# The low halves of the second product's input lie at other distances from their high halves

## Chip, core and metric

The kernel runs on one core of a Trainium2 chip. The metric is the device time of one execution in microseconds. Of the kernel before there are two timed executions, 2079.07 and 2080.16 us, median 2079.61.

## What is computed

Attention with four sink positions and a window of 128 (batch 4, 8 heads, 768 positions, 64 wide) gives a matrix `x` of 3072 tokens by 512. It goes through a soft mixture of 8 experts, whose weights per token come from eight rounds of normalizing rows and columns:

```python
def _moe_ref(x, w_gate, w1, w2):          # x: 3072 x 512, w1: 8 x 512 x 1024, w2: 8 x 1024 x 512
    ...                                    # P: 3072 x 8, weights of the experts
    for e in range(E):
        h = np.maximum(x @ w1[e], 0.0)     # first product
        ye = h @ w2[e]                     # second product
        out += P[:, e:e + 1] * ye
```

Nearly all of the time goes into the two products of the mixture.

## The kernel before

**Tiling.** After the attention the 3072 tokens are taken in three parts of 1024. The code counts them 0, 1 and 2; here they are parts 1, 2 and 3. An expert's 1024 inner columns are taken in four units of 256, so a part has 8 x 4 = 32 units. Both products go by Strassen's scheme on blocks of 2 by 2: seven products `M1` to `M7` in place of eight, with sums of blocks before and after.

**Halves.** A value in float32 is kept as two numbers of the type that TensorE multiplies at full rate: a high half, which is the value cast, and a low half, which is the value less its high half. A product then takes three matmuls: high by high, high by low, low by high. A tile that holds both is `[128, 2, n]`: along each partition first the n high numbers and then the n low ones. With n = 512 in float32 the low half starts 2048 bytes after the high one.

**Parts 2 and 3.** `first2` (from L1392) makes the first product of a unit. Each of the seven `M` is six matmuls of 512 columns (line L902, in `product`), whose weights come from the queue `W1q` and whose streaming operand is one of the token forms `B11`, `B21`, `B22`, `T1` to `T4`. ScalarE copies a result out of its bank (L1411), VectorE adds another to it (L1415) and takes the positive part times the expert's weight (L1416, L1445), GpSimd makes three sums and differences (L1434, L1438, L1439, L1449). That gives the seven forms of the second product's input: `A11`, `A12`, `A22`, `S1` to `S4`, each 128 partitions by 512 tokens.

`form` (L1418) gives each form a tile `hf` of the pool `hq`, which has 16 buffers and is the last pool opened on its side of the on-chip memory. `piece` (L926) writes it: ScalarE casts the source into the high half (L928), and one step later VectorE subtracts this high half from the source into the low half (L931). A part makes 32 x 7 forms, both parts 448.

`second2` (from L1456) makes the second product. For each group of two units, each `M` and each of its two halves of output columns `k`, it has three matmuls a unit (L1467); the streaming operand is a half of `hf`, the weights come from `W2q`:

```python
for j, (a, w, n) in enumerate((a, w, n) for n in group for a, w in ((0, 0), (0, 1), (1, 0))):
    nc.tensor.matmul(o, lhsT=W2Q[part, n, m][:, a, k * P:(k + 1) * P], rhs=F[part, n, H_OF[m]][:, w, :],
```

`w` = 0 is the high half and `w` = 1 the low one, so of three matmuls the second streams a low half. A result goes to VectorE (L1481), which adds it to a sum in on-chip memory, or stays in a bank of its own (`held`) over several groups.

**Order.** The order is written out by hand: a unit's steps are listed in `STEPS2`, and `at(n, f)` puts an operation n steps later. A form is written in one unit and read in later ones.

**Part 1** has the same two products with other tiles: L902 with weights `W1f`, and L1152, whose streaming operand is a half of the weights `W2f`. Before all of it stands the attention, beside which the first expert's plain products run (L638, L652).

One place of the attention is used below. The scores' keys lie in `KQ`, a tile `[P, 2, NP, CW + 2 * P]` with NP = 2 and rows of 260 + 256 = 516 floats; L498 streams the first 260 (or 132) floats of such a row:

```python
KQ = [att1.tile([P, 2, NP, CW + 2 * P], F32R, name=f"KQ{hh}") for hh in range(2)]
    for j, (a, c) in enumerate(terms):         # ((0, 0), (0, 1), (1, 0))
        for r in range(2):
            rows = slice(r * D, (r + 1) * D)
            nc.tensor.matmul(..., lhsT=Q[rows, a, pr, :], rhs=K[rows, c, pr, 0:w], ...)
```

So L498 goes in pairs (`r`), one matmul for each half of the partitions. L473 and L474 write the high and low halves of `KQ` from the transposed keys and queries, 512 elements a partition in four blocks of 128.

Of the kernel before, what the change touches and what calls it, by code (L numbers as in the profile page):

```python
# [2 lines left out]

# [7 lines left out]
F32R = mybir.dt.float32r  # L11
# [5 lines left out]
P = 128  # L17
# [221 lines left out]
def tile_sink_attention_moe(ctx: ExitStack, tc: tile.TileContext, q, k, v, wg, w1, w2, out):  # L239
# [14 lines left out]
    HT = NPART // 2  # L254
# [128 lines left out]
    for hh in range(2):  # L383
        t = att2.tile([P, NP, CW + 2 * P], F32, name=f"KQF{hh}")
# [514 lines left out]
    def product(ps, w1, x, start, stop):  # L899

        for j, (a, k, b) in enumerate(TERMS):
            nc.tensor.matmul(ps, lhsT=w1(a, k), rhs=x[:, b, k, :], start=(start and j == 0),  # L902
                             stop=(stop and j == len(TERMS) - 1), skip_group_check=not start)
# [9 lines left out]
    def at(steps, f):  # L913
        assert steps > 0
        due.setdefault(clock[0] + steps, []).append(f)
# [10 lines left out]
    def piece(dst, src, then=None):  # L926

        nc.scalar.copy(dst[:, 0], src)  # L928

        def low():  # L930
            low_ = nc.vector.tensor_sub(dst[:, 1], src, f32(dst[:, 0])).ins  # L931
            if clock[0] < 120:
                LATE[:] = [tc, low_]

        at(1, low)
        if then:
            at(3, then)
# [398 lines left out]
    with ExitStack() as p1:  # L1336
        pool_ = lambda name, bufs, **kw: p1.enter_context(tc.tile_pool(name=name, bufs=bufs, reuse_waits="tile", **kw))
        W1N, W2N = 8, 16
        w1p, pb, cp, wp, hp = pool_("w1q", W1N), pool_("pb", 2), pool_("cq", 1), pool_("wq", 6), pool_("hq", 16)
        ORDER = ["M2", "M1", "M5", "M3", "M6", "M7", "M4"]  # L1340
        units1 = [(e, u) for e in range(E) for u in range(NU)]
        NJ = len(units1)
# [3 lines left out]
        W2Q = {}  # L1346
        coming1 = iter([(part, n, m) for part, n in jobs1 for m in ORDER if (part, n, m) not in W1Q])
        first_ones = set(W1Q)

        def load_w1(k):  # L1350
            for _ in range(k):
                key = next(coming1, None)
                if key:
                    part, n, m = key
                    t = W1Q[key] = w1p.tile([P, 2, KH, P], F32R, name="W1q")
                    nc.sync.dma_start(f32(t).rearrange("p w k f -> p w (k f)"), w1s[units1[n]][:, FA[W1_OF[m]]])
# [28 lines left out]
        def load_form(m):  # L1385
            fm = READS[m]
            XF[fm] = (xpool if fm[0] == "B" else xtp).tile([P, 2, KH, HT], F32R, name=fm)
            nc.sync.dma_start(f32(XF[fm]), xfs[FORMS.index(fm)])

        F = {}  # L1390

        def first2(part, n):  # L1392

            PB = PBS[part, units1[n][0]]
            T = {}

            def run(m):
                c = "c2" if m in ("M2", "M5", "M3") else "c1"
                start = m in ("M2", "M1", "M5")
                if start:  # L1400
                    T[c] = ps0.tile([P, HT], F32, name=c)
                W = W1Q.pop((part, n, m))
                product(T[c], lambda a, k: W[:, a, k, :], XF[READS[m]], start, True)
                if (part, n, m) not in first_ones:
                    at(1, lambda: load_w1(1))
                if (part, n) == (1, NJ - 1):
                    at(1, lambda: load_form(m))

            def copied(m):
                t = T[m] = cp.tile([P, HT], F32, name=m)  # L1410
                nc.scalar.copy(t, T["c2"])  # L1411

            def summed(key, m, th):
                w = T[key] = wp.tile([P, HT], F32, name="w")
                nc.vector.tensor_add(w, T["c1"], T[m])  # L1415
                nc.vector.scalar_tensor_tensor(w, w, 0.0, PB[:, th], op0=ALU.max, op1=ALU.mult)  # L1416

            def form(steps, fm, src):  # L1418
                def f():
                    t = F[part, n, fm] = hp.tile([P, 2, HT], F32R, name="hf")  # L1420
                    piece(t, src)

                at(steps, f)

            def after(m):
                if m in ("M2", "M5", "M3"):
                    copied(m)
                elif m == "M1":
                    summed("A11", "M2", 0)
                    form(2, "A11", T["A11"])  # L1430
                elif m == "M6":
                    summed("A21", "M3", 1)
                    S3 = wp.tile([P, HT], F32, name="w")
                    nc.gpsimd.tensor_sub(S3, T["A11"], T["A21"])  # L1434
                    form(2, "S3", S3)
                elif m == "M7":
                    summed("A22", "M5", 1)
                    nc.gpsimd.tensor_add(T["A21"], T["A21"], T["A22"])  # L1438
                    nc.gpsimd.tensor_sub(T["A11"], T["A21"], T["A11"])  # L1439
                    form(2, "S1", T["A21"])  # L1440
                    form(3, "A22", T["A22"])
                    form(4, "S2", T["A11"])
                else:
                    w = wp.tile([P, HT], F32, name="w")
                    nc.vector.scalar_tensor_tensor(w, T["c1"], 0.0, PB[:, 0], op0=ALU.max, op1=ALU.mult)  # L1445
                    form(1, "A12", w)

                    k = 4 if n < 2 else 3
                    at(k, lambda: nc.gpsimd.tensor_sub(T["A11"], w, T["A11"]))  # L1449
                    form(k + 2, "S4", T["A11"])  # L1450

            return run, after
# [190 lines left out]
```

## Time and profile before

| | |
|---|---|
| timed executions | 2079.07 and 2080.16 us, median 2079.61 |
| profiled execution, span from first to last instruction | 2077.3 us |
| its own time outside the span | not given; the median of the timed ones is 2.3 us above the span |
| TensorE busy | 2060.9 us, 99% of the span |
| VectorE busy | 1462.4 us, 70% |
| ScalarE busy | 840.2 us, 40% |
| GpSimd busy | 713.7 us, 34% |
| L1467, matmuls of the second product in parts 2 and 3 | 1920 + 768 |
| L931 into `hf`, low halves | 448, 329.1 us |
| L928 into `hf`, high halves | 448, 265.3 us |

PE is TensorE's matmul, PEld its weight load, DVE VectorE, ACT ScalarE, POOL GpSimd. A matmul's duration in the trace overlaps with that of the next one, so its pace is read from starts: from the start of a group in the timeline to the start of the group after it, divided by the number in the group.

### The profile page before, as it was taken

The numbers are of one execution on the slowest core, as the hardware profiler recorded it, in microseconds if no ns is written. First come the engines' busy times: TensorE is split into PE (matmuls) and PEld (weight loads), VectorE is DVE, ScalarE is ACT, GpSimd is POOL, SyncE is SP. The second block draws the span as 40 slices with busy tenths as digits, with TensorE's granted clock in tenths as the row PEclk, the third lists the DMA queues.
The fourth block names the chain that finished last, engine by engine and source line by source line (L and its number), as shares of the span: only waits on it lengthen the run. The fifth ranks groups of instructions, "written<-read, shape, count | busy, mean of one in ns | idle before, by whom it ended". The sixth has DMA issues, their size and how long they took to land.

```text
span 2077.3 us, 31257 instructions
## 1 busy us (share of the span) xinstructions
PE 2060.9 (99%) x10407; PEld 1706.0 (82%) x10407; DVE 1462.4 (70%) x2732; ACT 840.2 (40%) x1787; POOL 713.7 (34%) x833
## 2 busy tenths in 40 slices
PE   8999999999999999999999999999999999999998
PEld 7888778888888888888888888888888888888887
DVE  6777688787877767756666666666666667666666
ACT  7877445444444444333323322332432232333222
POOL 7766523333333321322322232233332223222323
PEclk9999999999999999999999999999999999999999
DMA  7655269898989886766666666668766666666662
GB/s 178 161 118 120 85 211 323 288 319 291 315 282 323 289 274 223 280 211 197 199 203 198 204 205 191 202 207 334 224 208 194 200 205 191 207 203 202 197 193 83
DMA packets 397622, 453.78 MB, mean 218 GB/s; under 512 B 99664, under 2 KB 265744, under 8 KB 396560
## 3 DMA queue, kind: packets, MB, share of 16 engines
q1 hardware_dynamic: 397064, 451.57, 69.6%
q8 instruction: 85, 1.39, 0.3%
q14 instruction: 81, 0.66, 0.1%
q10 hardware_dynamic: 392, 0.16, 0.0%
HBM read 314.17 MB, written 137.46 MB: 217 GB/s over the span
## 4 chain that ended last, share of the span: by engine, by line
PE 96%; DVE 2%; ACT 1%; POOL 0%; issue 0%; DMA 0%; SPq 0%; DVEq 0%; ACTq 0%; POOLq 0%
PE c L902 42%; PE o L1467 21%; PE held L1467 8%; PE held L1152 7%; PE o L1152 7%; PE st L638 2%; PE st L652 2%; PE st L572 2%; PE st L498 2%; PE st L457 1%; PE st L530 1%; PE st L580 0%; DVE sc L508 0%; DVE st L507 0%; PE st L603 0%
## 5 line engine op out<-in xcount | busy, mean ns | idle before, releaser
L928 ACT CAST hf<-w 128x512 fp32r<-128x512 f32 x448 | 265.3, 621 | 562.2 <-POOL w L1434 299.7
L1467 PE MATMUL o<-hf,W2q 128*128 128x512 f32 x1920 | 472.0, 389 | 0.0
L1467 PEld LDWEIGHTS o<-hf,W2q 128*128 128x128 f32 x1920 | 360.0, 188 | 75.5 <-DVE acc L1481 0.9
L902 PE MATMUL c<-T,W1q 128*128 128x512 f32 x1530 | 388.8, 389 | 0.2 <-DVE w L1415 0.2
L931 DVE TENSOR_TENSOR hf<-w,hf 128x512 fp32r<-128x512 f32 x448 | 329.1, 763 | 75.6 <-ACT hf L928 68.0
L902 PEld LDWEIGHTS c<-T,W1q 128*128 128x128 f32 x1530 | 286.8, 188 | 60.7 <-DVE w L1415 0.9
L1481 DVE TENSOR_TENSOR acc<-o,acc 128x512 f32<-128x512 f32 x298 | 204.6, 687 | 169.9 <-PE o L1467 169.9
L902 PE MATMUL c<-B,W1q 128*128 128x512 f32 x1134 | 278.3, 389 | 0.0
L1434 POOL TENSOR_TENSOR w<-w 128x512 f32<-128x512 f32 x64 | 82.7, 1293 | 492.0 <-DVE w L1416 492.0
L902 PEld LDWEIGHTS c<-B,W1q 128*128 128x128 f32 x1134 | 212.5, 188 | 44.0
L1415 DVE TENSOR_TENSOR w<-c,M 128x512 f32<-128x512 f32 x192 | 132.2, 689 | 139.9 <-PE c L902 135.6
L1411 ACT COPY M<-c 128x512 f32<-128x512 f32 x192 | 112.8, 587 | 249.1 <-PE c L902 249.0
L1467 PE MATMUL held<-hf,W2q 128*128 128x512 f32 x768 | 194.8, 389 | 0.0
L1152 PE MATMUL held<-W2f,h 128*128 128x512 f32 x672 | 171.1, 390 | 0.0
L902 PE MATMUL c<-T,W1f 128*128 128x512 f32 x672 | 171.0, 390 | 0.1
L1152 PE MATMUL o<-W2f,h 128*128 128x512 f32 x672 | 170.5, 389 | 0.1
L1467 PEld LDWEIGHTS held<-hf,W2q 128*128 128x128 f32 x768 | 144.0, 188 | 29.8
L1449 POOL TENSOR_TENSOR w<-w 128x512 f32<-128x512 f32 x64 | 106.3, 1661 | 176.0 <-DVE hf L931 176.0
L1152 PEld LDWEIGHTS o<-W2f,h 128*128 128x128 f32 x672 | 126.0, 188 | 27.0 <-DVE acc L1159 0.9
L902 PEld LDWEIGHTS c<-T,W1f 128*128 128x128 f32 x672 | 125.8, 188 | 26.9 <-issue 0.5
L1152 PEld LDWEIGHTS held<-W2f,h 128*128 128x128 f32 x672 | 125.8, 188 | 26.4 <-DVE W2f L931 0.5
L961 POOL TENSOR_TENSOR r<-r 128x256 f32<-128x256 f32 x27 | 20.1, 745 | 367.8 <-ACT M L1115 231.4
(216 smaller groups left out, 2740.3 us busy)
## 6 DMA issues: line engine op xcount, KB each, us to landing
W2q<-w2s SPq DMA_DIRECT2D x448, 256.0 KB, 3.1
W1q<-w1s SPq DMA_DIRECT2D x444, 256.0 KB, 2.8
w1s<-W1f SPq DMA_DIRECT2D x56, 896.0 KB, 7.7
w2s<-WT SPq DMA_DIRECT2D x136, 256.0 KB, 3.2
r<-in_moe_w_dram SPq DMA_DIRECT2D x64, 512.0 KB, 5.5
w2s<-W2f SPq DMA_DIRECT2D x56, 256.0 KB, 5.7
PB<-psd SPq DMA_DIRECT2D x16, 512.0 KB, 4.0
w2s<-W2f SPq DMA_DIRECT2D x56, 128.0 KB, 7.8
```

What stands on the lines that cost most here:

```text
L498: nc.tensor.matmul(ps[hh * HH + 2 * pr + r][:, 0:w], lhsT=Q[rows, a, pr, :], rhs=K[rows, c, pr, 0:w], start=(j == 0), stop=(j == len(terms ...
L572: nc.tensor.matmul(O[r * D:(r + 1) * D, c], lhsT=x_[:, 2 * c + r], rhs=y_[:, 2 * c + r], start=(j == 0 and c == 0), stop=(j == len(ops) - ...
L902: nc.tensor.matmul(ps, lhsT=w1(a, k), rhs=x[:, b, k, :], start=(start and j == 0), stop=(stop and j == len(TERMS) - 1), skip_group_check=n ...
L928: nc.scalar.copy(dst[:, 0], src)
L931: low_ = nc.vector.tensor_sub(dst[:, 1], src, f32(dst[:, 0])).ins
L1152: nc.tensor.matmul(o, lhsT=h[c, th][:, a, off:off + P], rhs=W2F[n][:, w, c, :], start=(begin and c == 0 and j == 0), stop=(end and c == 1 ...
L1411: nc.scalar.copy(t, T["c2"])
L1415: nc.vector.tensor_add(w, T["c1"], T[m])
L1434: nc.gpsimd.tensor_sub(S3, T["A11"], T["A21"])
L1449: at(k, lambda: nc.gpsimd.tensor_sub(T["A11"], w, T["A11"]))
L1467: nc.tensor.matmul(o, lhsT=W2Q[part, n, m][:, a, k * P:(k + 1) * P], rhs=F[part, n, H_OF[m]][:, w, :], start=(j == 0 and (begin or not hol ...
L1481: nc.vector.tensor_add(sums[m, k], o, sums[m, k])
```

## The change

The tile of a form grows from 1024 to 1040 floats a partition, 4160 bytes in place of 4096, so that the 16 buffers of `hq` lie 4160 bytes apart. The low half begins 512, 516 or 520 floats after the high half, by turns from form to form in the order in which the forms are made. The high half still begins at the start of its buffer. The shapes of all operations on the halves remain 128 by 512, each of contiguous floats. No instruction is added, removed or moved on any engine, and the waits are the same. Tiles of other pools keep their places.

```diff
+        gaps = itertools.cycle((0, 4, 8))
+
+        def new_h():
+
+            gap = next(gaps)
+            t = hp.tile([P, 2 * HT + 16], F32R, name="hf")
+            return t[:, 0:2 * (HT + gap)].rearrange("p (w c) -> p w c", w=2)[:, :, 0:HT]
+
...
             def form(steps, fm, src):
                 def f():
-                    t = F[part, n, fm] = hp.tile([P, 2, HT], F32R, name="hf")
+                    t = F[part, n, fm] = new_h()
                     piece(t, src)
```

HT is 512.

## Rows read from the trace of the kernel before

**Rows 1.** Page and cores: span, busy us (share) xinstructions; span and granted clock.
```profile
span 2077.3 us, 31257 instructions
PE 2060.9 (99%) x10407; PEld 1706.0 (82%) x10407; DVE 1462.4 (70%) x2732; ACT 840.2 (40%) x1787; POOL 713.7 (34%) x833
core 0: 2077.3 us, clock 0.999
```

**Rows 2.** Page: the chain that ended last, by engine and by line.
```profile
PE 96%; DVE 2%; ACT 1%; POOL 0%; issue 0%; DMA 0%; SPq 0%; DVEq 0%; ACTq 0%; POOLq 0%
PE c L902 42%; PE o L1467 21%; PE held L1467 8%; PE held L1152 7%; PE o L1152 7%; PE st L638 2%; PE st L652 2%; PE st L572 2%; PE st L498 2%; PE st L457 1%; PE st L530 1%; PE st L580 0%; DVE sc L508 0%; DVE st L507 0%; PE st L603 0%
```

**Rows 3.** Busy time by stretch, 866 to 2062: all; then `hf` alone; `W1q` alone.
```profile
866.00:2062.00 1196.00, 1195.77 (x5288) 988.97 (x5287) 804.31 (x1181) 375.02 (x650) 362.49 (x261) 1.00 0.66 206
...
866.00:2062.00 1196.00, 655.44 (x2669) 500.50 (x2669) 320.26 (x436) 257.84 (x435) 1.00 0.66 206
...
866.00:2062.00 1196.00, 637.83 (x2587) 484.75 (x2586) 1.00 0.66 206
```

**Rows 4.** Waits of PE, 866 to 2062, all there are: us, times, longest.
```profile
PE c L902 <- DVE w L1415: 0.2, 1, 0.2
```

**Rows 5.** Timeline of PE (start, us, engine, line), around 1002 and around 801.
```profile
1000.67 1.52 PE L902 MATMUL c<-B,W1q 128*128 128x512 f32 x6
1002.03 1.52 PE L1467 MATMUL held<-hf,W2q 128*128 128x512 f32 x6
1003.39 0.84 PE L902 MATMUL c<-T,W1q 128*128 128x512 f32 x3
...
800.37 1.52 PE L1152 MATMUL o<-W2f,h 128*128 128x512 f32 x6
801.73 1.52 PE L1152 MATMUL held<-W2f,h 128*128 128x512 f32 x6
```

**Rows 6.** Lines by form, 866 to 2062: xcount | busy us, mean ns | idle before.
```profile
L931 DVE TENSOR_TENSOR hf<-w,hf 128x512 fp32r<-128x512 f32 x436 | 320.3, 762 | 74.7 <-ACT hf L928 67.1
L1481 DVE TENSOR_TENSOR acc<-o,acc 128x512 f32<-128x512 f32 x296 | 203.3, 687 | 169.8 <-PE o L1467 169.8
L1415 DVE TENSOR_TENSOR w<-c,M 128x512 f32<-128x512 f32 x186 | 128.1, 689 | 137.1 <-PE c L902 132.8 <-issue 3.0 <-ACT M L1411 1.4
L1534 PE MATMUL o<-ident,acc 128*128 128x128 f32 x32 | 4.8, 272 | 0.0
```

**Rows 7.** Timeline of PE: a run on `KQ`, from its second pair, its last two pairs.
```profile
74.10 1.70 PE L498 MATMUL st<-KQ 64*128 64x260 f32 x24
...
74.32 0.40 PE L498 MATMUL st<-KQ 64*128 64x260 f32 x4
...
75.40 0.40 PE L498 MATMUL st<-KQ 64*128 64x260 f32 x4
```

**Rows 8.** Timeline of PE before 55; line L638's durations there: ns min/median/max.
```profile
53.81 1.36 PE L638 MATMUL st<-B,W 128*128 128x256 f32 x10
...
L638 PE MATMUL st<-B,W x48: 278/283/333, 42.1 to 54.9; 128*128 128x256 f32 x48
```

**Rows 9.** Tile `hf`: ns min/median/max, first and last start; who waited for it (us, times).
```profile
L1467 PE MATMUL held<-hf,W2q x768: 389/389/478, 866.0 to 2065.9; 128*128 128x512 f32 x192
L928 ACT CAST hf<-w x448: 612/622/634, 836.5 to 2051.8; 128x512 fp32r<-128x512 f32 x150
L931 DVE TENSOR_TENSOR hf<-w,hf x448: 673/683/1245, 838.0 to 2054.5; 128x512 fp32r<-128x512 f32 x150
...
  POOL w L1449: 176.0, 64
  DVE acc L1481: 169.9, 174
```

**Rows 10.** Tile `KQ`: ns min/median/max of the writes of its halves.
```profile
L473 ACT CAST KQ<-st x36: 578/589/601, 52.2 to 212.2; 128x512 fp32r<-128x512 f32 x36
L474 DVE TENSOR_TENSOR KQ<-st,KQ x36: 676/686/692, 52.8 to 213.0; 128x512 fp32r<-128x512 f32 x36
```

More of the change, by code (lines that the diff above doesn't have):

```diff
@@ L1 @@
+import itertools
 import math
```

## The prediction

> **What bounds the kernel now.** I read the page from the top. TensorE is busy for 99% of the span of 2077.3 us, and its granted clock is 0.999, the upper of its two levels, 2.4 GHz [rows 1]. The chain that ended last is TensorE for 96% of the span, and 29% of it is the line that the change feeds, L1467 (21% into `o`, 8% into `held`) [rows 2]. Then I cut out the stretch in which parts 2 and 3 do both products, 866 to 2062 us. TensorE is busy for 1195.77 of its 1196 us, and in all that time it waits for another engine once, 0.2 us [rows 3, 4]. So nothing that VectorE, ScalarE, GpSimd or the DMA queues do in it is late by more than that; what sets the time is the pace of the matmuls.
>
> The pace is read from starts in the timeline. Six matmuls of 512 columns on `hf` start at 1002.03 and the next line starts at 1003.39: 1.36 us, 0.2267 us each. The same six-fold step of 1.36 us stands at the first product in the same place (1000.67 to 1002.03) and in part 1's second product (800.37 to 801.73), where the streaming operand is `W2f`, not `hf` [rows 5]. In the stretch 2669 matmuls on `hf` and 2587 on `W1q` were recorded [rows 3]; (2669 + 2587) x 0.2267 = 1191.4 us. With 4.8 us for the 32 transposes in between [rows 6] this is 1196.2, the whole stretch: there is only pace in it.
>
> **The change part by part.** In both programs each engine has the same instructions in the same order with the same waits. Only addresses differ: the 448 high writes, the 448 low writes (which also read the high half), and 2688 matmuls that stream a half (448 forms x 2 x 3). The pool `hq` is the last one opened on its side, so no other tile moves, and 16 buffers grow by 64 bytes each. The gap goes 0, 4, 8 floats by turns, so 298 of 448 forms have a low half that begins 16 or 32 bytes past where it would. Each low half is streamed by two matmuls, hence 596 of the 896 low reads are moved against their high half. All 2688 reads lie at a new distance from the weights and from the other buffers, since a buffer is 4160 bytes and not 4096.
>
> *The matmul that streams a moved low half.* The trace has reads of this kind, in the attention. `KQ` is `[P, 2, NP, CW + 2 * P]` with rows of 516 floats, 2064 bytes, and L498 streams from the start of such rows: 0, 2064, 4128 and 6192 bytes past the tile's start, so 0, 16, 32 and 48 bytes past multiples of 2048. Wherever the tile begins, half of these starts lie off any grid of 32 bytes. The matmuls come in pairs, one on each half of the array's rows, 12 pairs in a run. The second pair of a run starts at 74.32 and the eleventh at 75.40 (the row of the last four): nine steps in 1.08 us, 0.120 us a pair of 260 columns [rows 7]. Against it stand ten matmuls of 256 columns whose streams start at multiples of 1024 bytes within their tile (L638): they fill 1.36 us, the last of them 0.28, so nine steps take 1.08 us, 0.120 each [rows 8]. The same pace with four columns more. With timestamps to 0.01 us in nine steps I can miss about 2 ns a pair; if only half of the starts paid, that is 4 ns each, and if the price grows with columns, 8 ns for 512. So the low reads cost between 0 and 596 x 8 ns = 4.8 us. I take 0.
>
> A gain from below: 256 columns fewer make a matmul 226.7 - 120.0 = 106.7 ns shorter, which is one column in each cycle of 2.4 GHz. So 512 columns need 213.3 ns, 256 need 106.7, and either matmul has the same 13.3 ns on top, a fixed rest [rows 5, 8]. The most that an address can give back without touching the column rate is that rest: 596 x 13.3 ns = 7.9 us for the moved low reads, 2688 x 13.3 = 35.8 us if every read of `hf` were freed of it. I take 0, since the rest is the same in L902, L1152 and L638 with quite other pairs of addresses.
>
> Here a rule and the row differ. The Trainium skill, TensorE: Matmul & The Clock Gate, section Back-to-back issue gap, gives 518 cycles for 512 columns at the warm clock, an estimate of 215.8 ns; this trace shows 226.7 ns throughout. By the page's figure the second product's matmuls would have 2688 x 10.9 ns = 29.3 us to win back, to about 2050 us; by the rows the surplus is not tied to `hf`, and the sum goes by the rows.
>
> *The low write (L931).* 448 subtractions, 673 ns at least, 683 median, 1245 at most [rows 9]. The nearest row with 16-byte shifts is L474, which writes the low half of `KQ`, also of 512 elements a partition: 676/686/692 ns [rows 10]. Additions whose operands keep their addresses take 687 and 689 [rows 6]. Price: 0. From above: if each took the longest time that was seen, 1245 instead of the mean of 762, the 436 in the stretch would add 211 us to VectorE's 804 of 1196 [rows 3, 6, 9]; that makes 1015, and VectorE still would not bound. What hides it is lead time: the first low half is written at 838.0, and the first matmul on `hf` comes at 866.0. TensorE isn't among those who wait for `hf` at all; GpSimd is, at L1449, with 176 us over 64 times [rows 9]; what it makes is one more form, which goes the same long way. Without that cover a write 0.5 us longer would cost up to 0.5 us a form.
>
> *The high write (L928)* begins at a multiple of 64 bytes as before, 612/622/634 ns [rows 9], price 0. It and L931 reuse buffers in the same order after the same reads, since no wait changed.
>
> *Sum.* 596 low reads x 0 + 448 low writes x 0 + 448 high writes x 0 = 0. The span stays 2077.3 us. The median of the two timed runs is 2079.61, 2.3 us above the span; the profiled execution's own total isn't given apart from its span, so I put these 2.3 us down to what lies around it and leave them: 2079.6.
>
> **The rivals.** *Faster: reads collide today.* High and low half lie 2048 bytes apart and the buffers 4096, so that a streamed half might meet a write or a weight load in the same part of the memory, and the fixed rest of 13.3 ns would be its price. Then the shift of the low half gives 7.9 us, 2071.7, and freeing all of `hf` 35.8 us, 2043.8. For it: the rest is there, and it is unexplained. Against: it is the same for 256 columns as for 512, where a collision along a read should cost more in the longer one, and the same for `W2f`, for the forms of the tokens (`B`, `T`) and for `hf`. Even whole, this stays within 2%.
>
> *Slower: a start off a coarser grid costs the stream.* It would have to act on full-height matmuls only, since the pairs of L498 show nothing, and they use half of the array's rows each; that difference is what is left for it. The point from which it decides is 2% of 2079.6, 41.6 us, over 596 reads: 70 ns each, 297 instead of 227. If a moved read took its columns at half the rate, 213.3 ns more, 596 x 213.3 = 127.1 us: 2206.7. L498 at half rate would need over 0.21 us a pair and shows 0.120 [rows 7]. The Trainium skill, SBUF — State Buffer, section Specifications (TRN2), speaks of lines of 16 bytes and of a price for an access that crosses into a new one; all three gaps are multiples of 16, so by that rule a half of 2048 bytes touches as many lines as before and the rival falls. No run here shows those lines by themselves.
>
> *Slower writes that surface.* L931 gets longer with a shifted output, and L1449 and the high writes behind it come later. It costs nothing until lead time is used up; with 0.5 us in every low write I see at most 1 to 2 us at the two part ends, about 2081. Against: L474's row.
>
> That the change doesn't do what it says is no rival here: the distances follow from the tile's shape and the slice.
>
> **How the numbers follow.** Forecast (addresses without price, 2077 to 2083 by the runs' own spread and the small bounds) 0.89; faster by a collision freed, 2043 to 2076, 0.05; slower reads 0.05, of which beyond the 41.6 us 0.02; late writes 0.01. The low end is 2074, between the forecast and the 7.9 us of the moved reads; the high end is 2088, which takes in the 4.8 us from L498 and as much again for the half-height pairs. About 2% is what a measurement of this kernel can tell from no change. Faster by over 2% would need more than the whole fixed rest of the second product (35.8 of 41.6 us): 0.01. Slower by over 2%: 0.02. Within: 0.97.
>
> **What would show it.** Right: the step from six matmuls on `hf` to the next line stays 1.36 us; the stretch 866 to 2062 keeps its length within 1 or 2 us; L931 stays at 683 median and L928 at 622; TensorE's waits in the stretch stay under 1 us. The collision rival shows as steps of 1.28 to 1.33 us on L1467 with L902 still at 1.36. The slow rival shows as L1467 alone stretching, in two forms out of three, and only in the second of each three matmuls. Late writes show as a wait of TensorE for L931. I am wrong if L902, whose operands don't move at all, changes its pace: then an address of `hf` acts on reads elsewhere, and I have no row for that.

## The result and the profile after

The changed kernel takes 2099.4 us (2099.07 and 2099.74), the kernel before 2079.61. The ratio is 1.0097, interval 1.0067 to 1.0126: 20 us slower, which is 1% and outside the range of 2074 to 2088. The interval lies above 1 as a whole, so the loss is clear of the noise. The forecast of no change was wrong.

The page and the two views that carried the forecast, for the changed kernel (its lines stand 1 lower at `product`, 9 lower in `second2`: L903 answers to L902, L1476 to L1467, L929 and L932 to L928 and L931):

```profile
span 2097.3 us, 31257 instructions
PE 2081.1 (99%) x10407; PEld 1706.1 (81%) x10407; DVE 1465.6 (70%) x2732; ACT 840.0 (40%) x1787; POOL 715.1 (34%) x833
PE 95%; DVE 2%; ACT 1%; POOL 0%; issue 0%; DMA 0%; SPq 0%; DVEq 0%; ACTq 0%; POOLq 0%
```

The chain that ended last is still TensorE, 95%. TensorE's busy time grew by 20.2 us (2060.9 to 2081.1) and so did the span (20.0, against [rows 1]); no other engine gained more than 3.2 us. The waits of TensorE in the old stretch of 866 to 2062 us, all there are, and the writes of the tile `hf` (ns min/median/max, first and last start):

```profile
PE c L903 <- DVE w L1424: 0.2, 1, 0.2
```

```profile
L929 ACT CAST hf<-w x448: 612/622/633, 836.3 to 2072.0; 128x512 fp32r<-128x512 f32 x150
L932 DVE TENSOR_TENSOR hf<-w,hf x448: 673/684/1253, 837.9 to 2074.6; 128x512 fp32r<-128x512 f32 x150
```

Against [rows 4, 9] nothing moved: one wait of 0.2 us, medians of 622 and 684 ns. The writes are not where the time went. It went into the pace. Busy time in the same stretch of `hf` and then of `W1q`, with the number of matmuls:

```profile
866.00:2062.00 1196.00, 649.66 (x2588) 485.45 (x2588) 316.49 (x431) 254.87 (x430) 1.00 0.67 206
...
866.00:2062.00 1196.00, 642.96 (x2581) 483.74 (x2580) 1.00 0.67 206
```

In the same 1196 us 5169 matmuls fit where 5256 did [rows 3]. Without the 4.8 us of transposes that is (1196 - 4.8) / 5169 = 230.4 ns a matmul against 226.6, and 3.8 ns x 5376 matmuls = 20.4 us. From the starts in the two traces, line by line in this stretch: matmuls on `hf` went from 226.7 to 231.9 ns, and those on `W1q`, none of whose operands moved, from 226.7 to 229.4. (2688 x 5.2 + 2688 x 2.7) ns = 21 us, a third of it on a line that the change doesn't touch.

A piece of the timeline of TensorE (start, us, line):

```profile
1207.83 1.55 PE L903 MATMUL c<-T,W1q 128*128 128x512 f32 x6
1209.21 1.55 PE L1476 MATMUL held<-hf,W2q 128*128 128x512 f32 x6
1210.60 2.91 PE L903 MATMUL c<-B,W1q 128*128 128x512 f32 x12
1213.35 1.52 PE L903 MATMUL c<-T,W1q 128*128 128x512 f32 x6
1214.71 1.55 PE L1476 MATMUL held<-hf,W2q 128*128 128x512 f32 x6
```

Six matmuls take 1.38, 1.39, then twelve 2.75, and then six take 1.36 again, the old step [rows 5], when eighteen matmuls of the first product stand in a row. The single steps between starts in this piece are, in ns: on `hf` 233, 225, 238, 227, 227, 236; on `W1q` 229, 231, 231, 236, 228, 232, 231, 227, 227, 226, 227, 227 and from there 226 and 227 only. Here seven steps of the first product are uneven behind the last matmul on `hf`. So a disturbance outlives its cause by several matmuls, and where the products alternate in sixes the second comes back before it has died away.

### The profile page after: what moved, and what is told of

Read it like the earlier page. It is cut to its first block, busy times and chain, and to the rows that moved or that the text cites. A ratio compares the mean times of both kernels' runs of the same rounds, so it can differ in the third digit from the quotient of the medians.

```text
span 2097.3 us, 31257 instructions
## 1 busy us (share of the span) xinstructions
PE 2081.1 (99%) x10407; PEld 1706.1 (81%) x10407; DVE 1465.6 (70%) x2732; ACT 840.0 (40%) x1787; POOL 715.1 (34%) x833
## 3 DMA queue, kind: packets, MB, share of 16 engines
q8 instruction: 85, 1.39, 0.3%
## 4 chain that ended last, share of the span: by engine, by line
PE 95%; DVE 2%; ACT 1%; POOL 0%; issue 0%; DMA 0%; SPq 0%; DVEq 0%; ACTq 0%; POOLq 0%
PE c L903 42%; PE o L1476 21%; PE held L1476 8%; PE held L1153 7%; PE o L1153 7%; PE st L653 2%; PE st L639 2%; PE st L573 2%; PE st L499 2%; PE st L458 1%; PE st L531 1%; DVE sc L509 0%; PE st L581 0%; DVE st L508 0%; PE st L604 0%
## 5 line engine op out<-in xcount | busy, mean ns | idle before, releaser
L929 ACT CAST hf<-w 128x512 fp32r<-128x512 f32 x448 | 265.4, 621 | 566.2 <-POOL w L1443 302.8
L1476 PE MATMUL o<-hf,W2q 128*128 128x512 f32 x1920 | 481.4, 394 | 0.0
L1476 PEld LDWEIGHTS o<-hf,W2q 128*128 128x128 f32 x1920 | 360.1, 188 | 83.7 <-DVE acc L1490 0.5
L903 PE MATMUL c<-T,W1q 128*128 128x512 f32 x1530 | 392.7, 392 | 0.2 <-DVE w L1424 0.2
L932 DVE TENSOR_TENSOR hf<-w,hf 128x512 fp32r<-128x512 f32 x448 | 329.2, 763 | 65.3 <-ACT hf L929 57.1
L903 PEld LDWEIGHTS c<-T,W1q 128*128 128x128 f32 x1530 | 286.9, 188 | 65.6 <-DVE w L1424 0.9
L903 PE MATMUL c<-B,W1q 128*128 128x512 f32 x1134 | 281.3, 392 | 0.0
L903 PEld LDWEIGHTS c<-B,W1q 128*128 128x128 f32 x1134 | 212.6, 188 | 48.1
L1476 PE MATMUL held<-hf,W2q 128*128 128x512 f32 x768 | 198.7, 394 | 0.0
L903 PE MATMUL c<-T,W1f 128*128 128x512 f32 x672 | 170.9, 390 | 0.1
L1476 PEld LDWEIGHTS held<-hf,W2q 128*128 128x128 f32 x768 | 144.0, 188 | 32.8
L903 PEld LDWEIGHTS c<-T,W1f 128*128 128x128 f32 x672 | 125.9, 188 | 26.9 <-issue 0.5
```

## The experiments

The lines of the two products stand a few lines apart from run to run; `c<-...,W1q` is always the first product and `hf,W2q` the second. The theories at the start: **A**, a streaming operand that starts off a multiple of 256 bytes costs its matmul some ns and leaves those behind it uneven. **B**, the distance between a form's halves or between buffers is what counts. **C**, the writes of ScalarE and VectorE at new places disturb TensorE's reads. A came from the trace of after: where three even steps stand ahead of a high half, the step of that half stays at 226.7 if its buffer lies at a multiple of 256 bytes (every fourth does, since 4160 = 16 x 256 + 64), and is about 237, 234 or 233 if it lies 64, 128 or 192 past.

**The spacing alone** (`e1_spacing`, from after):

```diff
-        gaps = itertools.cycle((0, 4, 8))
+        gaps = itertools.cycle((0,))
```

> The change's spacing alone: buffers 4160 bytes apart, every low half exactly 2048 bytes after its high half. Theory A (absolute start: a matmul whose streaming operand starts off a multiple of 256 bytes takes 6 to 10 ns longer, and the matmuls after it, aligned ones too, keep an uneven pace near 231 ns until it settles): three buffers of four lie 64, 128 or 192 bytes off, so most of the loss is there, 2094 to 2101 us, with the line of the second product near 232 ns and the first product's line in the same stretch near 229. Theory B (the distance between the two halves is what counts): 2079 to 2081 us, pace 226.7 everywhere. Theory C (shifted writes of ScalarE and VectorE disturb TensorE's reads): like A in time, but with slow matmuls only beside those writes.

Measured: 2099.36 us, ratio 1.0099 (1.0082 to 1.0116); from the starts 231.5 ns on `hf`, 229.4 on `W1q`. The whole loss without any gap between the halves. B in its first form falls; slow steps stand in every part of a unit, not beside the writes alone: the 2315 steps of the stretch during which an `hf` is being written take 230.4 ns on average, the 2846 others 230.6. Three buffers of four, with both halves in them, lie off a multiple of 256 bytes here.

**The pool moved by 64 bytes, all distances within it kept** (`e2_shift64`, from the kernel before):

```diff
-        w1p, pb, cp, wp, hp = pool_("w1q", W1N), pool_("pb", 2), pool_("cq", 1), pool_("wq", 6), pool_("hq", 16)
+        w1p, pb, cp, wp = pool_("w1q", W1N), pool_("pb", 2), pool_("cq", 1), pool_("wq", 6)
+        pool_("padq", 1).tile([P, 16], F32, name="padq")
+        hp = pool_("hq", 16)
```

> The kernel before with the whole pool of forms moved up by 64 bytes: distances between halves and between buffers are as before, every high and low half starts 64 bytes past a multiple of 256. Theory A (absolute start): all 2688 matmuls on the forms pay, up to 10 ns each, 27 us, and the first product's matmuls behind them lose some: 2099 to 2115 us. Theory B (distance of the halves or buffers): 2079 to 2081 us. Theory C (writes): the distance of the writes from all other reads has changed by 64 bytes only; 2079 to 2090 us.

Measured: 2098.34 us, ratio 1.0093 (1.0076 to 1.011). Halves and buffers stand to each other as before, and the loss is there: B is out. A's 27 us are too many: though every read is off, `hf` runs at 230.3 ns and `W1q` at 230.7. Timeline of TensorE:

```profile
1210.40 2.93 PE L902 MATMUL c<-B,W1q 128*128 128x512 f32 x12
1213.17 1.52 PE L902 MATMUL c<-T,W1q 128*128 128x512 f32 x6
1214.53 1.55 PE L1469 MATMUL held<-hf,W2q 128*128 128x512 f32 x6
1215.92 1.55 PE L902 MATMUL c<-B,W1q 128*128 128x512 f32 x6
1217.31 1.55 PE L1469 MATMUL o<-hf,W2q 128*128 128x512 f32 x6
```

Twelve aligned matmuls behind `hf` take 2.77 us, 50 ns more than 12 x 226.7. So a good part of the price is paid behind the off starts, by matmuls that are aligned themselves.

**All starts at multiples of 256 bytes, all distances changed** (`e4_gap256`, from after; the pool `b12` is closed before these pools open, so that there is room):

```diff
-        gaps = itertools.cycle((0, 4, 8))
+        gaps = itertools.cycle((0, 64))
...
-            t = hp.tile([P, 2 * HT + 16], F32R, name="hf")
-            return t[:, 0:2 * (HT + gap)].rearrange("p (w c) -> p w c", w=2)[:, :, 0:HT]
+            t = hp.tile([P, 2 * HT + 64], F32R, name="hf")
+            return Halves(t[:, 0:HT], t[:, HT + gap:2 * HT + gap])
```

> The low half lies 0 or 256 bytes past its old place by turns, buffers 4352 bytes apart, so every start is again a multiple of 256 bytes while all distances differ from before (the pool that stood above is closed a little earlier to make room). Theory A (absolute start): 2079 to 2082 us and a pace of 226.7 ns. Theory B (the distances of halves and buffers count): slower by much of the 20 us, 2090 to 2100 us. Theory C (writes at new places): slower too, 2085 to 2100 us.

Measured: 2078.98 us, ratio 1.0001 (0.9991 to 1.001); six matmuls on `hf` from 1211.38 to 1212.74, the old 1.36 us. Moved halves, moved buffers and moved writes cost nothing as long as they move by multiples of 256 bytes. B falls once more, and C as it was forecast, by which any new place of a write costs; writes that move by fewer bytes are not tested by this run.

```profile
1210.02 1.52 PE L905 MATMUL c<-B,W1q 128*128 128x512 f32 x6
1211.38 1.52 PE L1486 MATMUL o<-hf,W2q 128*128 128x512 f32 x6
1212.74 1.52 PE L905 MATMUL c<-T,W1q 128*128 128x512 f32 x6
```

**The gaps alone** (`e5_gaponly`, from after, with the same room made):

```diff
-            t = hp.tile([P, 2 * HT + 16], F32R, name="hf")
+            t = hp.tile([P, 2 * HT + 64], F32R, name="hf")
```

> The change's gaps alone: low halves 0, 16 or 32 bytes past their old place by turns, buffers 4352 bytes apart, so that all high halves start at multiples of 256 bytes. Theory A (absolute start): only the 596 moved low reads pay directly, 6 to 9 ns, and the ones after them lose some: 2086 to 2098 us, between before and the change. Theory B (distance between the halves): all of the 20 us, 2098 to 2101 us. Theory C (writes): 2085 to 2100 us.

Measured: 2097.06 us, ratio 1.0087 (1.007 to 1.0104). Now only 596 of the 5376 matmuls have an off start, and nine tenths of the loss are there. 18 us over 596 is 30 ns for each, of which its own step holds 6 to 9 and the ones behind it the rest. Where three even steps stand ahead, a low read moved by 16 bytes takes 232.5 ns on average and one moved by 32 bytes 235.8. Either part of the change makes nearly all of the loss, 20 us the spacing and 18 the gaps, and together they make no more than 20. That no even pace is left to break then is the likely reason; no run shows it by itself.

**Matmuls alone** (`e6_bench`). One block after another with constant starts, no other engine at work:

```python
for j in range(60):
    o = ps.tile([P, 512], F32, name="o") if j % 6 == 0 else o
    a, b = [4][j % 1], 0 + j % 6 * 128          # stream start, weight start, in numbers of 4 bytes
    nc.tensor.matmul(o[:, 0:512], lhsT=w[:, b:b + 128], rhs=x[:, a:a + 512], start=j % 6 == 0, stop=j % 6 == 5)
```

> Leaves out the whole computation: matmuls alone, one after another, six to a bank, in blocks that differ in where the streaming operand (or the weights) starts, with blocks of starts at multiples of 256 bytes between them; no other engine touches the memory meanwhile. Theory A1 (each start off a multiple of 256 bytes pays every time): blocks of 60 with 16, 32, 64, 128 and 192 bytes keep 232 to 237 ns, blocks at 0, 256, 512 and 1024 keep 226.7. Theory A2 (a change of the start is what costs; a row of equal starts finds its even pace again): blocks with one constant start fall back to 226.7 after 10 to 20 matmuls, the block that alternates 0 and 64 stays near 231, and one single off start among 35 aligned ones costs about 50 ns in all, spread over the ten after it. Theory C (other engines' accesses are needed for the slowdown): 226.7 in every block. Weights: unknown; if TensorE's weight reads have the same grid, the blocks with weights 64 or 128 bytes off are slow too.

Its timeline. L40, L50, L60 and L90 stream from 16, 32, 64 and 256 bytes, the blocks of 36 from 0; L150, L155 and L160 have weights 64, 128 and 256 bytes off; L130 is a block of 36 whose first start alone is 64 bytes off; L170 and L175 are 256 columns from 0 and 64; L185, L190 and L195 stream two-byte numbers from 0, 32 and 64:

```profile
36.82 14.06 PE L40 MATMUL o<-x,w 128*128 128x512 f32 x60
50.72 8.35 PE L45 MATMUL o<-x,w 128*128 128x512 f32 x36
58.91 14.17 PE L50 MATMUL o<-x,w 128*128 128x512 f32 x60
72.91 8.36 PE L55 MATMUL o<-x,w 128*128 128x512 f32 x36
81.11 13.91 PE L60 MATMUL o<-x,w 128*128 128x512 f32 x60
94.86 8.37 PE L65 MATMUL o<-x,w 128*128 128x512 f32 x36
...
147.42 13.76 PE L90 MATMUL o<-x,w 128*128 128x512 f32 x60
161.02 8.32 PE L95 MATMUL o<-x,w 128*128 128x512 f32 x36
...
234.76 8.37 PE L130 MATMUL o<-x,w 128*128 128x512 f32 x36
242.96 2.88 PE L135 MATMUL o<-x,w 128*128 128x512 f32 x12
...
256.61 14.16 PE L150 MATMUL o<-x,w 128*128 128x512 f32 x60
270.61 14.12 PE L155 MATMUL o<-x,w 128*128 128x512 f32 x60
284.56 13.81 PE L160 MATMUL o<-x,w 128*128 128x512 f32 x60
298.21 8.32 PE L165 MATMUL o<-x,w 128*128 128x512 f32 x36
306.37 7.36 PE L170 MATMUL o<-x,w 128*128 128x256 f32 x60
313.56 7.23 PE L175 MATMUL o<-x,w 128*128 128x256 f32 x60
320.63 4.48 PE L180 MATMUL o<-x,w 128*128 128x256 f32 x36
324.96 13.12 PE L185 MATMUL o<-xb,wb 128*128 128x512 bf16 x60
337.92 13.11 PE L190 MATMUL o<-xb,wb 128*128 128x512 bf16 x60
350.87 13.11 PE L195 MATMUL o<-xb,wb 128*128 128x512 bf16 x60
```

From start to start: 13.90 us for sixty at 16 bytes, 231.7 each; 14.00 at 32, 233.3; 13.75 at 64, 229.2; 13.60 at 256, 226.7. So no other engine is needed and C is out: VectorE, ScalarE and GpSimd do nothing in these blocks, and the granted clock is 1.00. A2 is out as well, since constant off starts do not find 226.7 again, though its two other forecasts came true (0 and 64 in turn take 231.2 ns; a block of 36 with a single off start, L130, takes 8.20 us, an aligned one 8.16). But A is not right either: weights 64 bytes off (14.00 us, 233.3 ns) do the same with an aligned stream; weights 256 off, 13.65 with nine uneven steps at first, come back to 226.7. Matmuls of 256 columns go the other way, 7.07 us for sixty at 64 bytes against 7.19 at 0. Weights 128 bytes off: 13.95, 232.5. Two-byte numbers take 12.95 us for sixty, 215.8 each, at each of five stream starts (their weights were not moved).

**Every stream start against every weight start** (`e7_grid`), which brings in theory **D**: the distance between the two starts, modulo 256, counts.

```python
grid = [(s, r) for r in range(0, 64, 4) for s in range(0, 64, 4)]      # numbers of 4 bytes
for s, r in grid:
    for n in range(30):
        b = r + k % 6 * 128
        nc.tensor.matmul(o, lhsT=w[:, b:b + 128], rhs=x[:, s:s + 512], start=k % 6 == 0, stop=k % 6 == 5)
```

> Leaves out the whole computation: after 72 matmuls from aligned starts, blocks of 30 matmuls of 512 columns each, for every pair of a streaming start 0, 16, ..., 240 bytes and a weight start 0, 16, ..., 240 bytes past a multiple of 256; TensorE alone is at work. Theory A (each of the two starts must be a multiple of 256 for itself): 226.7 ns only at the pair 0, 0, and 228 to 234 elsewhere. Theory D (the two reads of TensorE meet in the same part of the memory, so that the distance between streaming start and weight start counts): equal paces along equal distances, 226.7 again where both are shifted alike, and some distances that come out below 226.7, down to the 215.8 that two-byte numbers showed.

Mean step of a block in ns, without its first eleven, worked out from the starts (rows: weight start in bytes, columns: stream start 0, 16, ..., 240; five of sixteen rows):

```
  0  226.7 232.0 233.4 233.3 233.3 231.1 233.3 231.1 232.0 233.3 234.4 231.1 233.3 234.8 233.3 226.7
 16  233.3 233.3 226.7 232.2 231.8 226.7 229.7 233.3 226.7 233.3 233.3 226.7 232.0 228.9 233.3 226.7
 32  233.3 233.3 226.7 232.0 233.4 233.3 233.3 231.1 233.3 231.1 232.0 233.3 234.4 231.1 233.3 234.8
 48  233.3 226.7 226.7 230.0 228.2 232.2 231.9 226.7 229.7 233.3 226.7 233.3 233.3 226.7 232.0 228.9
 64  233.3 234.8 233.3 226.7 226.7 232.0 233.4 233.3 233.3 231.1 233.3 231.1 232.0 233.3 234.4 231.1
```

The row of 32 is the row of 0 moved by two columns, but for one block (stream 16), and that of 64 is moved by four. So with weights at multiples of 32 bytes the distance counts, and the step is 226.7 at distance 0 in all eight of these rows, and at 240 in seven. With weights at odd multiples of 16 the distance counts too, but the pattern is another: distance 0 takes 230.0 ns (fourth number in the row of 48, and likewise in the six rows beyond; 233.3 in the row of 16), and 226.7 stands at distances of 64, 112, 160 and 224, and at 240 in seven of the eight rows. D's "226.7 again where both are shifted alike" is thus right for half of the weight starts and wrong for the other half, and the paces below 226.7 that it looked for did not come: 55 of 256 blocks have 226.7, none is below, the rest lie at 228 to 235. A is out. What a block settles to also depends on where it came from: stream 64 with weights 0 gave 229.2 in the blocks above and 233.3 here.

**Everything moved by 64 bytes** (`e8_all64`, from the kernel before), A against D in the whole kernel. `base` lies on the other side of the memory, which fills downwards: 48 floats more move what follows by 192 bytes down, which is 64 up modulo 256.

```diff
-    const.tile([P, 8], F32, name="pad")
+    const.tile([P, 24], F32, name="pad")
...
-    base.tile([P, 120], F32, name="base")
+    base.tile([P, 168], F32, name="base")
```

> The kernel before with everything that the products read moved up by 64 bytes (modulo 256): token forms, forms of the second product, both queues of weights, in all three parts. No streaming operand starts at a multiple of 256 bytes any more, but every distance between streaming operand and weights is a multiple of 256 as before. Theory A (the streaming start must be a multiple of 256 for itself): all three parts slow down, 2105 to 2140 us. Theory D (the distance between streaming start and weight start, modulo 256, counts): 2078 to 2082 us, pace 226.7 ns.

Measured: 2078.94 us, ratio 1.0001 (0.9991 to 1.0011), 226.7 ns on both lines. Not one stream of the products in the mixture starts at a multiple of 256 and nothing is lost:

```profile
1209.82 1.52 PE L902 MATMUL c<-B,W1q 128*128 128x512 f32 x6
1211.18 1.52 PE L1467 MATMUL o<-hf,W2q 128*128 128x512 f32 x6
1212.54 1.52 PE L902 MATMUL c<-T,W1q 128*128 128x512 f32 x6
```

**Only the weights moved** (`e9_weights64`, from the kernel before):

```diff
+            pool_("padw", 1, side="right").tile([P, 48], F32, name="padw")
             w2p, accq = pool_("w2q", W2N, side="right"), pool_("accq", 3, side="right")
```

> The kernel before with only the queue W2q moved by 64 bytes (modulo 256); all forms lie where they lay. Theory A (only the streaming start counts): 2079 to 2081 us. Theory D (the distance counts): as much loss as when the forms alone were moved by 64 bytes, 2092 to 2104 us, on both lines of products, since the first product's matmuls behind a second product's take about ten to settle.

Measured: 2104.24 us, ratio 1.0122 (1.0106 to 1.0139), the slowest of all, with every form and every write of a form where it was before. (The pool `accq` of VectorE's sums, which is opened behind the queue, moves with it; the blocks of matmuls alone lose their pace without any such pool.) A is out here too. D's range ends a little below the measured time. The shift of the weights makes the distance 192 and not 64, and in `e6_bench` weights 64 bytes off took 233.3 ns where a stream 64 bytes off took 229.2; here the line of the second product takes 233.2, in `e2_shift64` 230.3. Twelve matmuls on `hf` take 2.80 us, 233.3 each, and the six behind them 1.39:

```profile
1202.72 2.96 PE L1467 MATMUL o<-hf,W2q 128*128 128x512 f32 x12
1205.52 1.55 PE L902 MATMUL c<-T,W1q 128*128 128x512 f32 x6
1206.91 2.96 PE L1467 MATMUL o<-hf,W2q 128*128 128x512 f32 x12
```

**A search for something faster** (`e10_search`): the kernel's order of threes with drawn starts.

```python
for xh, xl, wh, wl in grid:                     # 250 draws
    for n in range(30):
        s, r = ((xh, wh), (xl, wh), (xh, wl))[k % 3]
```

> Leaves out the whole computation: 250 blocks of 30 matmuls in the kernel's order of threes (high by high, high by low, low by high), with four drawn starts in a block (high and low streams, high and low weights, multiples of 8 bytes), the first block with all four at multiples of 256. If some arrangement frees a matmul of the fixed rest, blocks near 216 ns appear and the kernel can be made faster by up to 4%; if 226.7 ns is a floor for four-byte numbers with these weights, no block comes below it and most lie at 228 to 234.

The first block, all starts alike, gives 226.7 ns without its first eleven steps. One of the 249 draws comes to 226.7 as well, the rest are above, half of them above 233. No arrangement here beats that of the kernel before.

**One off matmul, and the attention's pairs** (`e11_single`):

```python
a, b = 16 * (j == 12), j % 6 * 128 + 0          # and the like for weights, and for both
...
nc.tensor.matmul(o2[r][:, 0:260], lhsT=w[r * 64:r * 64 + 64, b:b + 128], rhs=x[r * 64:r * 64 + 64, a:a + 260], ...)
```

> Leaves out the whole computation: matmuls alone. First, among aligned matmuls of 512 columns, one whose stream, or weights, or both start 64 bytes off; if the stream of a matmul meets the weights that are loaded for the next one meanwhile, then stream and next weights shifted alike stay at 226.7 for that step, and shifted weights already change the step before; if it meets its own weights, stream and own weights shifted alike stay even. Then pairs of half-height matmuls of 260 columns, as in the attention, with streams 0, 16, 32, 48, 64 and 256 bytes off: if the attention's row could show the price, the pairs at 0 and 256 are faster than the others by several ns; if it could not, all pairs take the same 110 to 120 ns. Last, full-height matmuls of 260 columns at 0, 16, 32 and 48.

The first question stays open: one stream off adds 46 ns to its block of 36, one weight start off 20, stream and own weights shifted alike also 20, stream and next weights alike 53. A single change disturbs in each case, even where its own distance is kept, so whether a stream meets its own weights or the next ones cannot be read from it. The disturbance by the stream lasts eight steps, that by the weights about five. The second is answered. Pairs at half height from 0 (L91) and 16 bytes (L97), and full height from 0 (L131):

```profile
104.81 7.41 PE L91 MATMUL o<-x,w 64*128 64x260 f32 x120
112.03 7.38 PE L97 MATMUL o<-x,w 64*128 64x260 f32 x120
119.14 7.36 PE L103 MATMUL o<-x,w 64*128 64x260 f32 x119
...
156.31 7.28 PE L131 MATMUL o<-x,w 128*128 128x260 f32 x60
163.42 7.27 PE L136 MATMUL o<-x,w 128*128 128x260 f32 x60
170.53 7.36 PE L141 MATMUL o<-x,w 128*128 128x260 f32 x60
```

Sixty pairs take 7.22 us from aligned starts, a start-up of 0.1 us in it, and 7.11 from 16 bytes off; sixty full-height matmuls of 260 columns 7.11 and 7.11, and 7.20 from 32 bytes off. At this length no price above 2 ns a matmul is to be seen.

## Why the prediction was wrong

**What bounds the kernel** held: TensorE's pace sets the time, and all 20 us came through it, with no new wait. The low writes, the high writes and the order were rightly put at nothing: one wait of 0.2 us and medians of 622 and 684 ns, against [rows 4, 9].

**The step that failed is the price of the moved low read**, put at 596 x 0 with an upper end of 596 x 8 ns = 4.8 us, where the runs show 20 us. It failed in three ways.

First, the row that bounded it could not carry the bound. The pairs on `KQ` [rows 7] showed 0.120 us from starts at all remainders, and I read that as no price. In `e11_single` aligned pairs take 0.119 us too, once started. A row prices a start only if the same row with an aligned start is known to be faster, and at 260 columns it isn't. Nor was the comparison with 256 columns at full height [rows 8] a safe one: `e6_bench` gives those 119.8 ns aligned and 117.8 off, and `e11_single` gives 118.5 ns to 260 aligned columns, less than to 256. So the 13.3 ns that the prediction calls a fixed rest are not fixed, and two lengths at unlike addresses could not be set side by side.

Second, the price was laid on the moved matmuls alone. A moved read costs its own step 6 to 9 ns, and then up to ten steps behind it stay uneven, 30 ns for each moved read in `e5_gaponly`. With this a third of the loss falls on L903, which the change doesn't touch. The prediction named this as what would prove it wrong, and had no row for it.

Third, the sum has no term for the new spacing of the buffers. The prediction says that all 2688 reads lie at a new distance from the weights, and then prices 596 of them, by their distance from the high half. `e1_spacing` keeps that distance in every form and loses 20 us by the spacing alone; `e2_shift64` keeps it too and loses 19.

**"The rest is the same in L902, L1152 and L638 with quite other pairs of addresses"** was the sentence that made the zero look safe, and it was not so. In the kernel before, the token forms begin at byte 3072, `W1q` at 76800, `hf` at 119808 and `W2q` at 196096, each a multiple of 256, and all steps within them are multiples of 256 too (these places follow from the kernel's pools). For the products of the mixture these were many addresses but one distance, zero modulo 256. The even pace [rows 5] was a special case that the change was about to break, and I took it for a property of the matmul.

**The rivals.** "A start off a coarser grid costs the stream" had the sign, but not the place or the size: it was to be seen in the second of three matmuls alone, and 70 ns in each were named as what would take it past 2%. What decides is no grid of stream starts (`e8_all64` has none on the grid and loses nothing) but the distance to the weights, together with where the weights start (`e7_grid`). The rule on lines of 16 bytes, from the Trainium skill (SBUF — State Buffer, Specifications (TRN2)), with which I let this rival fall, says nothing of two reads at once, and no run here speaks against it. "Reads collide today" was the nearer picture turned round: the pace does depend on the starts of stream and weights together, but at distance zero, as the kernel had them, it is the best that any of 506 blocks showed (256 in `e7_grid`, 250 in `e10_search`). Its gain of 8 to 36 us wasn't there to be had. The sentence on 518 cycles (the Trainium skill, TensorE: Matmul & The Clock Gate, Back-to-back issue gap) fits another type of number: its estimate of 215.8 ns is what `e6_bench` measures for two-byte numbers, from every start tried. Four-byte numbers, the type of this kernel's products, have 226.7 at best.

**The range** reached up to 2088, by the 4.8 us and as much again (which would add up to 2089.2). It was worked out from a wrong bound and would have had to reach 2105 (`e9_weights64`) to hold what a shift by a few bytes can do here. The chances went by the same bound; a loss of 1% lies within 2%, but for no reason that the prediction had. That about 2% is the least that a measurement of this kernel can tell was too coarse: the interval of 1.0067 to 1.0126 tells 1%.

What stays open is the mechanism below this: which weight load a stream meets, why distances such as 240 bytes are also free, and why a row with weights at odd multiples of 16 has another pattern, in which distance 0 is not free. The runs show that the steady pace goes by the distance in either kind of row, and that nothing but TensorE is needed; that two reads meet in the same part of the memory is argued, not shown.

## What to carry to other kernels

Where TensorE runs without a gap and multiplies four-byte numbers, measure the step between starts before and after any change of a tile's size, pad or order in memory: of the whole kernels here only those with stream and weights at like remainders modulo 256 bytes had the step of 226.7 ns at 512 columns (remainders of 0 and of 64 were tried; alone, like remainders at odd multiples of 16 took 230), and pads of a multiple of 256 bytes kept it (`e4_gap256`). A row bounds the price of an address only together with the same row at the other address. And an edit that moves one read in nine (`e5_gaponly`, 18 us) can cost nearly as much as one that moves every second (`e2_shift64`, 19 us), if the pace needs up to ten matmuls to settle.

## What was not expected of the hardware

The pace of matmuls of four-byte numbers at 512 columns depends on the distance between the start of the streaming operand and that of the weights, modulo 256 bytes: 226.7 ns at distance 0 and a few others when the weights start at a multiple of 32 bytes, other distances and not 0 when they start at an odd multiple of 16, 228 to 235 at the rest, steady patterns that repeat every few matmuls. Two-byte numbers show none of it at five stream starts (215.8 ns, so that the four-byte type of this kernel, "full rate" in the section on the halves, runs 5% below them), nor do 260 columns to more than 2 ns. From a single shifted start among aligned ones on, the steps in `e6_bench` were 237, 241, 224, 231, 236, 228, 233, 230 and then 227, 226, 227 again.
